# Another written order for the attention, gating and dispatch stage, and 34 in place of 48 idle products ahead of the first expert

## The chip, the cores and the metric

The kernel runs on one core of one Trainium2 chip. The metric is the device time of one execution in microseconds (us), the median of several runs. The engines of the core are TensorE (PE; its weight loads are listed apart as PEld), VectorE (DVE), ScalarE (ACT), GpSimd (POOL) and SyncE (SP), which here only issues transfers. Each engine takes its instructions in the order in which they stand in its queue, and a wait at the head of a queue holds everything behind it.

## What is computed

Three layers stand behind one another, all in fp32, on 2304 tokens of 512 features:

```python
# attention: 4 batches, 8 heads, 576 positions, head size 64, a window of 128 positions
scores = scale * q @ k.T + bias            # bias falls with the distance, outside the window -1e9
attn = exp(scores - max); attn /= attn.sum()
x = (attn @ v) as 2304 x 512

# experts: each token goes to one of 8
e_idx = argmax(x @ w_gate)
gate = softmax(x @ w_gate)[e_idx] * sigmoid(x @ w_output_gate)[e_idx]
x[e] = gate * (relu(x[e] @ w1[e]) @ w2[e])

# gated layer
out = (silu(x @ w_gate2) * (x @ w_val)) @ w_out
```

## The kernel before

**Stages.** The kernel works in three stages. The first (about 0 to 147 us) does attention, finds each token's expert, and writes each token's row to that expert's list in device memory (`xs`). The second computes the experts one after another, the third the gated layer. The change touches the first stage and the step from it to the first expert.

**The written order.** The first stage runs over 18 blocks `j` of 128 tokens, each in two halves of four heads (`j.hf`), and over 9 pairs of blocks `u`. Its order isn't left to a scheduler: the string `ORDER` (L28) lists 617 steps, and the loop under `manual_schedule` (L807) issues them one by one. So each engine's queue holds its part of the steps in the order of the string. A step is a letter and its place:

- `q`, `i`, `v`, `R`, `z` are transfers on SP: rows of q and k, of v, of the first expert's weights, and zeros into `xs`.
- `T` turns q and k (PE, tile `tq`), `Q` copies them out of PSUM (tile `qk`), `S` makes the scores (PE, tile `s`), `C` selects those inside the window and `M` adds the bias (DVE), `E` takes the exponentials (four on ACT), `P` turns them (PE, tile `tp`), `p` copies them out (tile `pt`), `K` masks them on POOL (`affine_select`, tile `ptm`), `V` multiplies by the values (PE, tile `o`), and `x` copies the result out (tile `xt`).
- `N` makes the reciprocal sums. `G`, `l`, `F`, `f` make the gating logits (PE, copy, PE, DVE). For six groups of blocks, `g` picks the expert, `e` takes two exponentials, `b` counts the tokens of the group (its first instruction writes `gs`), `w` makes the weights, `r` (PE) and `k` (DVE) the token's place (`gsli`).
- `t` turns the attention result back to rows (PE, tile `tx`), `X` scales the rows (DVE, tile `xtok`), `a` appends the token's number, and `D` (POOL, L769) writes a block's rows to their places with an indirect transfer.
- `H` (ACT) and `L` (POOL, L795) split a weight tile of the first expert into a high and a low part.

**A star** behind `Q`, `p`, `x` or `l` puts that copy on DVE in place of ACT (L807 to L811); behind another letter it means nothing.

**The hand-over.** After the last step, L1416 to L1431 issue in this order: the load of the first expert's rows (`load_x(0)`, tile `xr`, on SP), which waits until all 18 `D` have landed; `expert_tables`, a count of the tokens of each expert (PE, tile `cnt_ps`, L854) and a chain of small DVE instructions on it; products of a tile of ones that nobody reads, held behind the last count (`keep_warm`); five parts of `token_order`, which lengthen the DVE chain; and `emit_xT(0)`, which turns the first expert's rows (PE, L1063), copies the high part (ACT, `xh`, L1064) and subtracts the low part (DVE, `xl`, L1065). The first expert's products (L1440) take `xh` four times, then `xl` four times, then `xh` four times for each slice of the result.

Of the kernel before, what the change touches and what calls it, by code (L numbers as in the profile page):

```python
# [25 lines left out]


ORDER = """  # L28
q0 i0 q1 T0.0 a2 B1 Q0.0 q2 S0.0 B0 T0.1 C0.0 Q0.1 q3 T1.1 M0.0 S0.1 Q1.1 E0.0 T1.0 C0.1 q4 T2.0 Q1.0 S1.1 M0.1
Q2.0 E0.1 T2.1 C1.1 S1.0 v0 M1.1 T3.1 Q2.1 C1.0 E1.1 P0.1 q5 P0.0 M1.0 S2.1 p0.1 S2.0 Q3.1 K0.1 T4.1 p0.0 C2.0  # L30
v1 P1.1 E1.0 K0.0 C2.1 T3.0 V0.0 R0 M2.0 V0.1 Q3.0 R1 M2.1 E2.0 S3.0 q6 S3.1 C3.0 p1.1 T5.1 x0* Q4.1 K1.1 P1.0
M3.0 Q5.1 T4.0 q7 p1.0 P2.0 N0 Q4.0 T5.0 K1.0 C3.1 E2.1 S4.0 M3.1 V1.0 C4.0 q8 Q5.0 p2.0 V1.1 M4.0 E3.1 K2.0
S5.0 T6.0 v2 C5.0 E3.0 S4.1 T6.1 R2 C4.1 Q6.0 P2.1 v3 x1* Q6.1 P3.0 p2.1 T7.0 M5.0 p3.0 P3.1 K2.1 R3 M4.1 E4.0
T7.1 S5.1 v4 K3.0 S6.0 C5.1 Q7.0 z0 p3.1 G0 N1 H0 C6.0 P4.0 K3.1 l0 M5.1 V2.0 E4.1 v5 V2.1 p4.0 M6.0 S6.1 v6
E5.0 K4.0 x2* S7.0 C6.1 q9 F0 Q7.1 P4.1 f0 E5.1 T8.0 V3.0 C7.0 g0 V3.1 Q8.0 R4 p4.1 P5.1 q10 E6.0 M7.0 K4.1 P5.0
T8.1 M6.1 S7.1 L0* H1 x3* p5.1 S8.0 C7.1 v7 Q8.1 r0 p5.0 b0 T9.0 E6.1 N2 P6.0 R5 K5.0 M7.1 V4.0 q11 C8.0 V4.1
Q9.0 K5.1 k0 E7.0 G1 x4* S8.1 M8.0 q12 e0 P6.1 l1 C8.1 p6.0 T9.1 p6.1 P7.0 M8.1 Q9.1 t1 K6.1 E8.0 T10.0 w0 q13
S9.1 S9.0 C9.1 Q10.0 K6.0 V5.0 E7.1 R6 X1 V5.1 L1* M9.1 H2 R7 P7.1 p7.0 L2* v8 x5* F1 H3 T10.1 C9.0 p7.1 S10.0
K7.0 E9.1 R8 G2 v9 f1 V6.0 K7.1 Q10.1 V6.1 l2 z1 M9.0 E8.1 L3* T11.1 x6* F2 P9.1 f2 Q11.1 S10.1 p9.1 v10 H4 t0
K9.1 C10.1 E9.0 P8.0 z2 X0 P8.1 a3 V7.0 C10.0 L4* H5 M10.0 V7.1 p8.1 E10.0 v11 g1 S11.1 T12.1 z3 K8.1 C11.1 p8.0  # L40
T11.0 Q12.1 P9.0 M10.1 Q11.0 P10.0 K8.0 H6 T12.0 x7* S11.0 p10.0 R9 M11.1 L5* H7 V8.0 q14 C11.0 H8 Q12.0 a0 V8.1
N3 p9.0 M11.0 L6* e1 t5 E11.0 x8* G3 K9.0 z4 S12.1 w1 E10.1 S12.0 X5 T13.0 b1 R10 l3 T13.1 C12.0 L7* H9 F3 q15
V9.0 E11.1 f3 V9.1 N4 K10.0 C12.1 Q13.0 P11.0 Q13.1 M12.1 z5 T14.1 L8* p11.0 P10.1 x9* Q14.1 T14.0 H10 t2 M12.0
a1 L9* S13.0 p10.1 X2 Q14.0 R11 S13.1 E12.1 K10.1 z6 t3 C13.1 T15.0 K11.0 C13.0 P11.1 E12.0 V10.0 M13.0 L10* R12
V10.1 p11.1 X3 R13 H11 N5 P12.0 x10* Q15.0 z7 L11* T15.1 p12.0 M13.1 P12.1 Q15.1 S14.0 K12.0 E13.1 S15.0 C14.0
q16 G4 K11.1 C15.0 p12.1 V11.0 l4 M15.0 H12 K12.1 V11.1 E13.0 M14.0 v12 L12* r1 F4 P13.1 H13 f4 q17 S15.1 p13.1
D1 k1 E14.0 S14.1 g2 P13.0 D0 T16.1 p13.0 v13 T16.0 x11* Q16.1 P14.0 K13.0 C15.1 E15.0 G5 R14 C14.1 V12.0 K13.1
v14 M15.1 e2 V12.1 l5 D5 Q16.0 w2 v15 P15.0 p14.0 T17.0 M14.1 K14.0 p15.0 t4 R15 Q17.0 F5 S16.1 v16 H14 D2 N6 f5
x12 S17.0 E14.1 v17 V13.0 C16.1 K15.0 M16.1 V13.1 E15.1 L13* C17.0 S16.0 X4 L14* P14.1 x13 C16.0 P15.1 p14.1 r2
D4 b2 p15.1 t8 k2 G6 X8 a4 t7 K15.1 l6 M16.0 t6 E16.0 F6 V15.0 D3 f6 X6 V15.1 E16.1 a6 K14.1 X7 T17.1 M17.0  # L50
P16.0 Q17.1 D7 t9 g3 p16.0 P16.1 x15 S17.1 D8 p16.1 b3 V14.0 E17.0 N7 C17.1 K16.0 V14.1 X9 P17.0 K16.1 M17.1 x14
r3 e3 p17.0 t10 D9 w3 E17.1 t13 V16.0 X13 D6 k3 G7 N8 P17.1 l7 X10 K17.0 t11 p17.1 t12 X11 H15 F7 K17.1 V16.1
X12 f7 a5 D13 x16 g4 V17.0 e4 D10 V17.1 b4 w4 r4 x17 D11 t15 k4 G8 X15 t14 a7 L15* l8 F8 X14 t17 a8 f8 t16 D15
g5 e5 D14 b5 r5 w5 D12 X16 k5 X17 D16 D17
""".split()


# [89 lines left out]
def attn_moe_glu_kernel(ctx, tc, q, k, v, w_gate, w_ogate, w1, w2, w2_gate, w2_val, w2_out, out, caps=CAPS):  # L147
# [66 lines left out]
    with ExitStack():  # L214
# [610 lines left out]
        ps_m = wctx.enter_context(tc.tile_pool(name="ps_m", reuse_waits="tile", bufs=8, space=PSUM))  # L825
# [241 lines left out]
        yr, x2 = {}, {}  # L1067
# [314 lines left out]
        S_P5, S_P1, S_U2, V1, V2, G1, SG1, SG2 = range(8)  # L1382
# [237 lines left out]
```

## Time and profile before

| what | before |
|---|---|
| median of 3 runs | 804.83 us (803.99 to 805.16) |
| the profiled execution | 804.16 us |
| its span, first to last instruction | 802.0 us |
| mean granted TensorE clock | 0.993 |
| instructions | 17462 |
| PE busy | 777.6 us (97%) |
| DVE busy | 667.0 us (83%) |
| ACT busy | 504.7 us (63%) |
| POOL busy | 115.2 us (14%) |

The span leaves out 2.16 us of the profiled execution's own time, and this execution lies 0.67 us under the median. Shares of the whole span say little on the first stage, which is less than a fifth of it; so the rows below are of stretches. In a row of the timeline the number in brackets is the time that the engine had been idle before the instruction, with what ended that. Ends of PE's products are modelled, and a PE that is busy may be one that waits inside a group.

### The profile page before, as it was taken

Reading aid. Unit: us, or ns where it says so; the run is one execution under the profiler, and the core shown is the slowest. Engines: PE = TensorE matmul, PEld = TensorE weight load, DVE = VectorE, ACT = ScalarE, POOL = GpSimd, SP = SyncE. Lnnn points to the kernel's source line nnn. Section 1 sums busy time; section 2 is a strip of 40 time slices with the busy share of each in tenths; the row PEclk is TensorE's granted clock in tenths of the full one; section 3 lists DMA queues with packets and bytes.
Section 4 is the critical chain, followed back from the end, with each engine's and each line's share of the span. In section 5 each row is a group of like instructions: output and inputs, shape, how many; then the busy total and the mean of one; then the engine's idle time right before and its main releaser. Section 6 shows DMA issues by size and latency. Waiting matters only on the chain.

```text
span 802.0 us, 17462 instructions
## 1 busy us (share of the span) xinstructions
PE 777.6 (97%) x6031; PEld 720.7 (90%) x6031; DVE 667.0 (83%) x1808; ACT 504.7 (63%) x1355; POOL 115.2 (14%) x212
## 2 busy tenths in 40 slices
PE   8999998999999999999999999999999999999994
PEld 6888785799999999899899999999999999999993
DVE  8799787696798898889999999999877898777643
ACT  6999883266566677768776766665544665455431
POOL 5466787000000000000000000040000002000003
PEclk9999999999999999999999999999999999999998
DMA  9989943798868789990343221223110113011102
GB/s 181 242 200 309 292 132 125 228 309 244 253 216 259 232 287 291 278 335 27 127 135 109 99 93 52 71 114 131 54 51 28 54 54 131 28 52 53 52 29 81
DMA packets 120815, 121.16 MB, mean 151 GB/s; under 512 B 63634, under 2 KB 79634, under 8 KB 120722
## 3 DMA queue, kind: packets, MB, share of 16 engines
q1 hardware_dynamic: 113184, 106.31, 44.6%
q0 software_dynamic: 2880, 9.48, 3.1%
q10 hardware_dynamic: 4658, 4.20, 1.5%
q8 instruction: 49, 0.80, 0.4%
q14 instruction: 44, 0.36, 0.1%
HBM read 89.23 MB, written 30.73 MB: 150 GB/s over the span
## 4 chain that ended last, share of the span: by engine, by line
PE 40%; issue 34%; DVE 11%; ACT 6%; DMA 4%; POOL 2%; ACTq 1%; DVEq 0%; POOLq 0%; SPq 0%
PE pa L1312 7%; PE oo L1335 6%; PE oh L1440 5%; PE pb L1312 5%; PE oy L1464 4%; PE o L612 3%; DVE w L462 2%; PE s L521 2%; POOL out_dram L1350 2%; DMA rawd<-in_moe_w_gate_dram 2%; ACT w L461 2%; PE tp L589 1%; PE oy L1253 1%; PE oh L1232 1%; DVE t L1087 1%
## 5 line engine op out<-in xcount | busy, mean ns | idle before, releaser
L1335 PE MATMUL oo<-xh,hw 128*128 128x512 f32 x432 | 133.3, 390 | 0.0
L1312 PE MATMUL pa<-w 128*128 128x384 f32 x630 | 127.8, 338 | 0.8 <-ACT wtmp L1173 0.6
L1312 PEld LDWEIGHTS pa<-w 128*128 128x128 f32 x630 | 112.2, 188 | 9.4 <-ACT wtmp L1173 1.3
L1350 POOL DMA_INDIRECT out_dram<-ob,oid x18 | 20.5, 1137 | 631.9 <-ACT ob L1173 506.8
L1464 PE MATMUL oy<-hh,w 128*128 128x384 f32 (+5 forms) x448 | 101.1, 312 | 0.0
L1312 PE MATMUL pb<-w 128*128 128x384 f32 x468 | 94.5, 336 | 0.0
L1335 PEld LDWEIGHTS oo<-xh,hw 128*128 128x128 f32 x432 | 79.6, 187 | 6.4
L1173 ACT ACTIVATE w<-w 128x256 fp32r<-128x256 f32 (+2 forms) x168 | 76.2, 461 | 14.2 <-DVE w L1200 10.5
L1335 PE MATMUL oo<-xl,hw 128*128 128x512 f32 x216 | 84.4, 391 | 0.0
L1312 PEld LDWEIGHTS pb<-w 128*128 128x128 f32 x468 | 82.7, 188 | 0.4 <-DVE wtmp L1388 0.3
L462 DVE TENSOR_TENSOR w<-raw,w 128x512 fp32r<-128x512 f32 x112 | 75.1, 678 | 8.2 <-ACT w L461 6.6
L1440 PE MATMUL oh<-xh,w 128*128 128x384 f32 (+5 forms) x448 | 79.1, 316 | 0.0
L1173 ACT ACTIVATE wtmp<-pa 128x384 f32<-128x384 f32 x72 | 35.4, 492 | 65.0 <-PE pa L1312 64.8
L1464 PEld LDWEIGHTS oy<-hh,w 128*128 128x128 f32 x448 | 75.8, 188 | 0.0
L461 ACT ACTIVATE w<-raw 128x512 fp32r<-128x512 f32 x112 | 67.6, 622 | 8.5 <-ACT y L1107 5.3
L1440 PEld LDWEIGHTS oh<-xh,w 128*128 128x128 f32 x448 | 70.5, 192 | 0.6 <-ACT xh L1064 0.4
L1173 ACT ACTIVATE w<-wraw 128x256 fp32r<-128x256 f32 x108 | 44.5, 414 | 41.7 <-PE pa L1312 26.1
L1464 PE MATMUL oy<-hl,w 128*128 128x384 f32 (+5 forms) x224 | 69.8, 312 | 0.0
L1388 DVE TENSOR_TENSOR wtmp<-pb,wtmp 128x384 f32<-128x384 f32 x72 | 40.1, 557 | 32.5 <-ACT wtmp L1173 26.4
L1385 DVE TENSOR_TENSOR wtmp<-wtmp 128x384 f32<-128x384 f32 x108 | 58.5, 554 | 6.1 <-ACT wtmp L1391 5.4
L575 ACT ACTIVATE p<-p,mn 128x128 f32<-128x128 f32 x144 | 55.9, 401 | 0.5 <-DVE mn L554 0.3
L1221 DVE TENSOR_TENSOR w<-wraw,w 128x256 fp32r<-128x256 f32 x108 | 44.3, 419 | 6.3 <-ACT w L1173 6.3
(258 smaller groups left out, 1609.8 us busy)
## 6 DMA issues: line engine op xcount, KB each, us to landing
raw<-in_moe_w_dram SPq DMA_DIRECT2D x128, 256.0 KB, 3.8
xs<-zrow SPq DMA_DIRECT2D x8, 774.0 KB, 7.2
rawd<-in_moe_w_gate_dram SPq DMA_DIRECT2D x24, 256.0 KB, 4.4
rawd<-in_moe_w_val_dram SPq DMA_DIRECT2D x24, 256.0 KB, 3.4
rawd<-in_moe_w_out_dram SPq DMA_DIRECT2D x24, 256.0 KB, 3.7
xh<-wo_s SPq DMA_DIRECT2D x24, 256.0 KB, 2.6
xl<-wo_s SPq DMA_DIRECT2D x24, 256.0 KB, 2.8
w<-ys SPq DMA_DIRECT2D x6, 768.0 KB, 7.5
```

What stands on the lines that cost most here:

```text
L461: nc.scalar.activation(out=s[:, 0, :], in_=t, func=AF.Copy)
L462: TT(out=s[:, 1, :], in0=t, in1=s[:, 0, :], op=ALU.subtract)
L575: last_exp[0] = nc.scalar.activation(out=pr[:, c, :], in_=pr[:, c, :], func=AF.Exp, bias=mn[:, c:c + 1], scale=-1.0, accum_out=sums[j][:, ...
L1173: nc.scalar.activation(out=out, in_=in_, func=AF.Copy)
L1221: TT(out=flat(w_at(s, j)[:, 1]), in0=w_src(s, j), in1=flat(w_at(s, j)[:, 0]), op=ALU.subtract)
L1312: nc.tensor.matmul(out=bank_of(j), lhsT=w[:, a, k, :], rhs=x_at(j, b, k), start=(n == 0 and j in (0, 1, 5)), stop=(n == 5), skip_group_che ...
L1335: nc.tensor.matmul(out=o_w[c], lhsT=h_at(s, t)[b][:, b0 * 128:b0 * 128 + 128], rhs=wo_at(s, a), start=(kk == 0 and i == 0), stop=(kk == KF ...
L1350: r = nc.gpsimd.indirect_dma_start(out=out[:, :], out_offset=bass.IndirectOffsetOnAxis(ap=oid[:, 2 * WB * pr + c, :], axis=0), in_=ob, in_ ...
L1385: TT(out=out, in0=a, in1=b, op=ALU.mult)
L1388: TT(out=temp(i), in0=bank_of(j), in1=temp(k), op=ALU.add)
L1440: nc.tensor.matmul(out=o[:, 0:n], lhsT=wt["w1", p, m // 4, kk][:, a, (m % 4) * 128:(m % 4) * 128 + 128], rhs=(xh, xl)[b][:, kk, :], start= ...
L1464: nc.tensor.matmul(out=o[d][:, 0:n], lhsT=wt["w2", p, 0, kk][:, a, d * 128:d * 128 + 128], rhs=(hh, hl)[b][:, kk, :], start=(kk == 0 and i ...
```

## The change

The string `ORDER` is written anew, with the same 617 steps in another order, and with stars on other copies: before, 12 copies are on DVE (`x0` to `x11`); after, 24 are (nine `Q`, nine `p`, `x2`, `x5`, `x8`, `x12`, `l2`, `l5`). Nothing is added or left out. The number of idle products goes from 48 to 34.

```diff
 ORDER = """
-q0 i0 q1 T0.0 a2 B1 Q0.0 q2 S0.0 B0 T0.1 C0.0 Q0.1 q3 T1.1 M0.0 S0.1 Q1.1 E0.0 T1.0 C0.1 q4 T2.0 Q1.0 S1.1 M0.1
+q0 i0 q1 T0.0 Q0.0 q2 T0.1 S0.0 Q0.1 S0.1 a3 C0.0 B0 v0 T1.1 M0.0 T1.0 Q1.1 q3 E0.0 C0.1 S1.1 a0 a2 T2.0 C1.1
...
-g5 e5 D14 b5 r5 w5 D12 X16 k5 X17 D16 D17
+D14 r5 t17 b5 D12 X16 k5 X17 D16 D17 L13* L14* L15*
 """.split()
...
         with tc.issue_after(last_cnt[0]):
-            keep_warm(ps_m, "m", 48)
+            keep_warm(ps_m, "m", 34)
```

Of POOL's queue, these are the last rows of the stage. `xs<-xtok,gsli` is a `D`, `w<-raw,w` an `L`, `apart` a small write that stands between two `D`, `zcols` the first instruction of the hand-over. Before:

```order
L642 COPY xtok<-pads 128x2x4
L795 TENSOR_TENSOR w<-raw,w 128x512
L642 COPY xtok<-pads 128x2x4
L769 DMA xs<-xtok,gsli 18433x516
L768 MEMSET apart 1x1
L769 DMA xs<-xtok,gsli 18433x516
...
L769 DMA xs<-xtok,gsli 18433x516
L837 MEMSET zcols 128x1664
```

and after:

```order
L642 COPY xtok<-pads 128x2x4
L769 DMA xs<-xtok,gsli 18433x516
L768 MEMSET apart 1x1
L769 DMA xs<-xtok,gsli 18433x516
...
L769 DMA xs<-xtok,gsli 18433x516
L795 TENSOR_TENSOR w<-raw,w 128x512 x3
L837 MEMSET zcols 128x1664
```

The last three splits (`L13` to `L15`) stood ahead of `D`s before, one of them five `D`s before the end; now all three run behind the last `D`.

On ACT, the end of the stage: `xt<-o` is an `x`, `lt<-g` an `l`, `w<-raw` an `H`, `geo` and `pe` an `e`. Before:

```order
L504 ACTIVATE xt<-o 128x4x128
L504 ACTIVATE lt<-g 128x256
L715 ACTIVATE geo<-lg 128x16
L716 ACTIVATE pe_209<-gsh 128x2x8
L1419 ACT_TABLE_LOAD
```

and after:

```order
L504 ACTIVATE xt<-o 128x4x128 x2
L786 ACTIVATE w<-raw 128x512 x2
L504 ACTIVATE lt<-g 128x256
L715 ACTIVATE geo<-lg 128x16
L716 ACTIVATE pe_209<-gsh 128x2x8
L1419 ACT_TABLE_LOAD
```

Two splits (`H14`, `H15`) now stand between the last `x` and the last `l`.

On DVE, the last group's gating, from the choice of the expert to the counts of the hand-over (`gs` and `gbase` are of `b`, `pe` to `gwi` of `w`, `xtok` is an `X`, `grk` to `gsli` are `k`). Before:

```order
L709 TENSOR_TENSOR gohb<-iota8m,gmn 128x16
L725 TENSOR_REDUCE gs<-gohb 128x8
L727 TENSOR_TENSOR expf<-gmn,iota8m 128x2
L729 TENSOR_TENSOR gbase<-expf,rows_e 128x2
L757 TENSOR_TENSOR pe_209<-gohb,geo 128x2x8
...
L762 TENSOR_TENSOR gwi<-inv,gwgt 128x16
L683 TENSOR_TENSOR xtok<-tx,gwi 128x512
```

and after:

```order
L709 TENSOR_TENSOR gohb<-iota8m,gmn 128x16
L757 TENSOR_TENSOR pe_209<-gohb,geo 128x2x8
...
L762 TENSOR_TENSOR gwi<-inv,gwgt 128x16
L725 TENSOR_REDUCE gs<-gohb 128x8
L727 TENSOR_TENSOR expf<-gmn,iota8m 128x2
L729 TENSOR_TENSOR gbase<-expf,rows_e 128x2
L683 TENSOR_TENSOR xtok<-tx,gwi 128x512
```

The group's count `gs`, on which the count of all tokens and with it the idle products wait, moves behind the five instructions of the weights. What follows (`L683` to the counts of the hand-over) is the same in both.

## Rows read from the trace of the kernel before

**Rows 1.** Busy time by stretch: PE, PEld, DVE, ACT, POOL, granted clock, DMA share, GB/s.

```profile
0.00:20.00 20.00, 17.07 (x276) 12.46 (x280) 16.67 (x80) 13.41 (x47) 10.28 (x55) 1.00 0.99 181
20.00:60.00 40.00, 39.52 (x819) 34.37 (x809) 33.93 (x165) 39.48 (x156) 22.34 (x32) 1.00 0.94 221
60.00:80.00 20.00, 19.31 (x339) 16.32 (x336) 18.86 (x73) 18.23 (x63) 13.97 (x20) 1.00 1.08 309
80.00:138.00 58.00, 52.46 (x858) 41.82 (x859) 46.54 (x208) 40.12 (x144) 43.69 (x66) 1.00 0.61 185
150.00:310.00 160.00, 160.00 (x1027) 159.52 (x1026) 132.01 (x301) 101.21 (x231) 0.00 (x0) 1.00 0.84 261
```

**Rows 2.** The chain of waits in the first stage: start, length, what.

```profile
11.52 0.96 ACT qk L504 x2
...
61.34 0.70 DVE s L542
...
115.90 1.79 DVE gbase L729
```

**Rows 3.** Groups by line and shape, 0 to 138 us: busy us, mean ns | idle before.

```profile
L504 ACT ACTIVATE qk<-tq 128x512 f32<-128x512 f32 x36 | 20.9, 592 | 5.4 <-PE tq L495 5.4
L786 ACT ACTIVATE w<-raw 128x512 fp32r<-128x512 f32 x16 | 10.0, 630 | 1.3 <-DMA raw<-in_moe_w_dram 1.3
L506 DVE COPY xt<-o 128x512 f32<-128x512 f32 x12 | 8.2, 686 | 0.6 <-PE o L612 0.5
```

**Rows 4.** Timeline of DVE and POOL at 72 to 77 us, gating of one group.

```profile
72.71 1.23 POOL L278 TENSOR_SCALAR_AFFINE_SELECT ptm<-pt 128x512 f32<-128x512 f32 x2
72.81 0.18 DVE L760 RECIPROCAL gwgt<-gwgt 128x4 f32<-128x4 f32 x1
...
73.90 1.27 POOL L795 TENSOR_TENSOR w<-raw,w 128x512 fp32r<-128x512 f32 x1
...
74.22 0.98 DVE L727 TENSOR_TENSOR expf<-gmn,iota8m 128x4 f32<-128x4 f32 x1
...
75.23 1.33 DVE L729 TENSOR_TENSOR gbase<-expf,rows_e 128x4 f32<-128x4 f32 x1
75.27 1.27 POOL L795 TENSOR_TENSOR w<-raw,w 128x512 fp32r<-128x512 f32 x1
```

**Rows 5.** Timeline of PE and ACT at the last values product.

```profile
126.26 1.97 PE L612 MATMUL o<-ptm,vr 128*64 128x128 f32 x32 [0.79 <-ACT geo L715]
...
129.81 0.60 ACT L504 ACTIVATE xt<-o 128x512 f32<-128x512 f32 x1 [3.23 <-PE tx L680]
...
131.17 0.38 ACT L504 ACTIVATE lt<-g 128x256 f32<-128x256 f32 x1 [0.76 <-PE g L648]
```

**Rows 6.** Timeline of the hand-over to the first expert, 134 to 150 us.

```profile
134.74 10.52 PE L250 MATMUL warm<-ones 128*128 128x512 bf16 x48
...
137.33 0.96 POOL L769 DMA_INDIRECT xs<-xtok,gsli  x1 [1.69 <-DVE gsli L750]
...
138.59 0.96 POOL L769 DMA_INDIRECT xs<-xtok,gsli  x1 [0.21 <-DVE reg L862]
139.57 0.94 DVE L876 TENSOR_TENSOR end<-end,held 128x1 f32<-128x1 f32 x5
...
146.16 1.69 PE L1063 MATMUL tx<-ident,xr 128*128 128x128 f32 x12 [0.90 <-DMA xr<-xs]
146.70 0.30 DVE L910 TENSOR_REDUCE lim<-tbl 128x18 f32<-128x144 f32 x1
...
147.32 1.95 DVE L1065 TENSOR_TENSOR xl<-tx,xh 128x384 fp32r<-128x384 f32 x4 [0.32 <-ACT xh L1064]
...
148.78 0.99 PE L1440 MATMUL oh<-xl,w 128*128 128x384 f32 x4
```

**Rows 7.** Busy time and granted clock around two pauses of PE, columns as Rows 1.

```profile
328.00:330.00 2.00, 0.41 (x3) 0.24 (x3) 1.97 (x5) 2.00 (x6) 0.00 (x0) 1.00 0.68 216
330.00:332.00 2.00, 2.00 (x12) 2.00 (x12) 1.97 (x5) 1.17 (x4) 0.00 (x0) 0.55 1.12 221
332.00:334.00 2.00, 2.00 (x13) 2.00 (x13) 0.31 (x1) 0.41 (x2) 0.00 (x0) 0.59 1.04 240
354.00:356.00 2.00, 0.79 (x7) 0.63 (x6) 1.97 (x6) 2.00 (x8) 0.00 (x0) 1.00 1.06 395
```

More of the change, by code (lines that the diff above doesn't have):

```diff
@@ L28 @@
 ORDER = """
-q0 i0 q1 T0.0 a2 B1 Q0.0 q2 S0.0 B0 T0.1 C0.0 Q0.1 q3 T1.1 M0.0 S0.1 Q1.1 E0.0 T1.0 C0.1 q4 T2.0 Q1.0 S1.1 M0.1
[L30 to L53, printed above, removed]
@@ L54 @@
-g5 e5 D14 b5 r5 w5 D12 X16 k5 X17 D16 D17
+q0 i0 q1 T0.0 Q0.0 q2 T0.1 S0.0 Q0.1 S0.1 a3 C0.0 B0 v0 T1.1 M0.0 T1.0 Q1.1 q3 E0.0 C0.1 S1.1 a0 a2 T2.0 C1.1
+Q1.0 P0.0 Q2.0 q4 T2.1 M0.1 E0.1 M1.1 S1.0 p0.0* S2.0 Q2.1 C1.0 R0 E1.1 K0.0 P0.1 C2.0 T3.1 q5 T3.0 M1.0 V0.0
+Q3.1 p0.1 P1.1 M2.0 E2.0 K0.1 S3.1 p1.1* q6 S2.1 Q3.0* K1.1 E1.0 V0.1 C2.1 T4.0 B1 C3.1 T4.1 Q4.0 v1 M2.1 P1.0
+Q4.1 P2.0 E2.1 M3.1 T5.0 R1 S3.0 p2.0* q7 S4.0 C3.0 Q5.0 T6.0 p1.0 C4.0 T5.1 K1.0 Q6.0 M3.0 P2.1 x0 T6.1 v2 M4.0
+E3.0 S4.1 K2.0 p2.1* S5.0 q8 Q6.1* K2.1 E4.0 V1.0 C4.1 V1.1 M4.1 E3.1 P4.0 R2 Q5.1* T7.0 C5.0 R3 P3.0 H0 S5.1 N0
@@ new lines @@
+x1 v3 p3.0* L0* H1 V2.0 C5.1 p4.0 v4 E4.1 M5.0 V2.1 K4.0 M5.1 S6.1 q9 K3.0 H2 Q7.0* S6.0 E5.0 C6.1 G0 L1* x2*
+T7.1 R4 l0 C6.0 P4.1 Q7.1 P3.1 R5 M6.1 p4.1 P5.0 p3.1 T8.0 z0 N1 E5.1 T8.1 M6.0 K3.1 S7.0 Q8.0* S7.1 K4.1 p5.0
+Q8.1* T9.0 E6.0 q10 C7.0 P5.1 L2* C7.1 F0 V3.0 Q9.0 M7.0 E6.1 V3.1 f0 v5 S8.0 g0 p5.1 R6 T9.1 x3 P6.1 K5.1 C8.0
+E7.0 v6 P6.0 M7.1 V4.0 K5.0 v7 p6.0* Q9.1 V4.1 e0 M8.0 K6.0 p6.1 v8 S9.0 x4 w0 E7.1 S8.1 q11 C9.0 T10.0 K6.1
+T10.1 Q10.0 P7.1 C8.1 Q10.1 P7.0 H3 V5.0 p7.1* q12 H4 L3* M9.0 V5.1 E9.0 M8.1 a1 S9.1 L4* x5* p7.0 R7 S10.1 C9.1
@@ new lines @@
+E8.0 K7.1 G1 q13 G2 V6.0 K7.0 H5 l2* C10.1 l1 E8.1 V6.1 N3 v9 M9.1 F2 P8.0 N2 E9.1 T11.0 f2 R8 S10.0 z1 p8.0*
+P9.0 Q11.0 C10.0 K8.0 T12.0 p9.0 M10.1 T12.1 Q12.0 T11.1 L5* x6 M10.0 F1 R9 S11.0 E10.0 Q11.1* v10 K9.0 S12.0
+Q12.1* V7.0 E10.1 f1 q14 V7.1 g1 e1 P10.0 x7 P8.1 C11.0 p10.0 T13.0 q15 b0 p8.1 P9.1 M11.0 H6 t0 K8.1 V8.0 E11.0
+X0 K10.0 C12.0 V8.1 z2 Q13.0 M12.0 S12.1 p9.1 E12.0 w1 S11.1 T14.0 R10 K9.1 C12.1 P10.1 Q14.0 z3 C11.1 t1 p10.1
+P12.0 X1 T14.1 K10.1 p12.0 M12.1 t5 Q14.1 P11.0 H7 M11.1 L6* r0 z4 S13.0 E12.1 x8* S14.0 b1 V9.0 k0 E11.1 R11 N4
@@ new lines @@
+V9.1 K12.0 C13.0 v11 p11.0 T13.1 X5 L7* P12.1 C14.0 Q13.1 q16 t3 p12.1 M13.0 T15.1 H8 r1 K12.1 M14.0 S14.1 H9 x9
+S13.1 N5 E13.0 z5 C14.1 L8* V10.0 X3 V10.1 k1 K11.0 E14.0 G3 z6 Q15.1* G4 l3 C13.1 L9* P13.0 H10 M14.1 P11.1 l4
+p13.0 t4 L10* p11.1 T15.0 z7 X4 t2 Q15.0 K11.1 M13.1 P14.0 x10 F3 S15.0 H11 f3 E13.1 v12 S15.1 L11* C15.0 V11.0
+C15.1 q17 p14.0 V11.1 M15.1 K13.0 T16.1 X2 x11 K14.0 T16.0 M15.0 Q16.1 P13.1 R12 Q16.0 F4 D4 N6 S16.1 E15.0 R13
+f4 S16.0 v13 g2 D0 G5 e2 E15.1 V12.0 v14 l5* D5 b2 V12.1 w2 v15 H12 D1 T17.1 p13.1 x12* P15.1 Q17.1 R14 T17.0
@@ new lines @@
+C16.1 K13.1 p15.1 r2 v16 Q17.0 P15.0 k2 E14.1 D2 F5 V13.0 f5 R15 V13.1 M16.1 a4 v17 p15.0 a6 K15.1 E16.1 P14.1
+C16.0 t6 D3 N7 t9 M16.0 x13 S17.0 p14.1 X9 K15.0 S17.1 E16.0 C17.0 G6 X6 L12* P16.1 C17.1 l6 P16.0 p16.1 K14.1
+t8 M17.1 H13 V15.0 E17.1 M17.0 a5 V15.1 K16.1 p16.0* t7 X8 x15 K16.0 F6 E17.0 V14.0 X7 f6 D9 V14.1 g3 e3 P17.1
+D6 x14 P17.0 p17.1 b3 G7 p17.0 w3 D8 t11 l7 t10 X11 r3 K17.0 X10 F7 V16.0 f7 D7 V16.1 k3 g4 t13 e4 t15 x16 t12
+X13 K17.1 V17.0 X12 D11 w4 V17.1 X15 t14 x17 a7 D10 r4 N8 H14 G8 X14 H15 b4 t16 l8 a8 k4 F8 D13 f8 g5 D15 e5 w5
```

## The prediction

> **What bounds the kernel now.** I read the busy time by stretch first [rows 1]. From 150 us on PE is busy all the time (160.00 of 160), so a delay or gain at the first expert passes to the end in full; what remains is the first stage and the hand-over. Up to 80 us the transfers take 0.94 to 1.08 of what the DMA engines have, and the compute engines are nearly full too: from 20 to 60 us PE 39.52 and ACT 39.48 of 40, DVE 33.93; from 60 to 80 us PE 19.31, DVE 18.86, ACT 18.23 of 20. Only the first 20 us (PE idle 2.9) and the end, 80 to 138 us (PE idle 5.5, counting idle products as work), have room. Then the chain of waits [rows 2]: early it runs over ACT (a piece is `qk`, 0.96 for two copies), later over DVE (`s`, and `gbase`, an instruction on 128x4 numbers that took 1.79 us). Last the hand-over [rows 6]: the last `D` is issued at 138.59, the expert's rows are there at 146.16, and the small DVE chain that began beside it ends at 147.00 (146.70 + 0.30), 0.32 us ahead of the first `xl`. So the DVE chain and the load end almost together.
>
> **The change part by part.** (1) Copies. Nine `Q` and nine `p` leave ACT, eight `x` come back, two `l` leave: 18 x 0.59 - 8 x 0.59 + 2 x 0.38 = 6.7 us less on ACT [rows 3, 5]. DVE gets ten more at 0.686 and two smaller at some 0.4: 7.7 us more. So the load isn't made smaller, it moves from an engine that was full early to one that had 85% in the stretch from 20 to 60 us. By their place in the string (an estimate, steps counted against the stretches) three of the 24 starred copies fall in the first 20 us, 13 in the 40 us after it (6 before), four in the next 20 (four before), four behind that (two before). In the first 20 us ACT makes the chain, and three copies less are worth up to 3 x 0.59 = 1.8 us, while DVE has 3.3 us of room: taken as -1.2. From 20 to 60 us seven more copies cost DVE 7 x 0.6 = 4.2 us of its 6.07 idle, and PE can't go faster than 39.52 of 40: 0. From 60 to 80 us nothing. Behind that the order sets the exponentials and value products against the row work anew; PE has 5.5 us of idle time there, of which a good part is the latency of the last blocks; nothing in the trace shows the new waits. Nearest bounds: all of PE's idle time in the stage goes (-6, some of it can't), or half of DVE's ten extra copies land where DVE makes the chain (+3). Taken: -0.8, nearer to nothing, since the work is the same. Parts of SP's queue move too (`v0`, `q3`, the zero fills); their sum is the same and DMA is full to 80 us either way; in the value above. Sum of (1): **-2.0**, from -6 to +3.
>
> (2) The end of attention. Two weight splits of 0.63 us on ACT now stand between the last `x` and the last `l` [rows 3]. Before, `l` began 0.76 us after `x` ended (129.81 + 0.60 to 131.17), the time of the product between them [rows 5]; now it can't begin before 2 x 0.63 = 1.26: **+0.5**. The last value products end at 128.23, and their copy begins only at 129.81 [rows 5]; the 1.58 us between have no cause that I see and may not come again: between 0 and -1.6, half taken, **-0.7**.
>
> (3) The three splits behind the last `D`. For the `D`s it is a gain of 3 x 1.27 us of POOL, but POOL waited 1.69 us for DVE ahead of the last two `D`s [rows 6], so that is worth 0. Behind them it costs. DVE instructions with two operands in SBUF stand still while POOL works on SBUF data [rows 4]: `expf` took 0.98 us and ended with POOL's split (73.90 + 1.27 = 75.17), `gbase` 1.33 us and ended with the next (75.27 + 1.27 = 76.54). The three splits run from the end of the last `D` (138.59 + 0.96 = 139.55 in before's time) for 3.8 us, just where DVE's chain does `end` (five in 0.94 us, undisturbed [rows 6]) and more of the kind. If one passes at the end of each split, the chain gets on by 3 x 0.19 = 0.6 us in 3.8, and loses 3.2. It had 0.32 us of slack, so the four `xl` come **2.9 us** later, and PE's second pass, which takes `xl` from 148.78 on [rows 6], with them. Queued behind on DVE: the `xl`, then the first `hl`; who waits is PE. Bounds: 0, if such narrow operands slip through, and 3.8 - 0.3 = 3.5, if none passes.
>
> An instruction with one operand ran at its usual length beside POOL, `gwgt` 0.18 us under a POOL instruction that began at 72.71 [rows 4]. The Trainium skill, GPSIMD Engine Reference, section Key points, says that GpSimd shares its SBUF interfaces with VectorE and gets in the way of instructions with two SBUF inputs and also of those in a two-port mode. By it single-operand copies of the chain might be held as well, which would give the upper bound, 806.0 in place of 805.4; the row with 0.18 us speaks against that here.
>
> (4) 34 idle products. One is 10.52 / 48 = 0.219 us [rows 6]. The group's count now stands behind five small instructions (0.94 us for five such), so the products begin 1.0 us later against the `D`s, and 34 of them end at 134.74 + 1.0 + 7.45 = 143.2 in place of 145.26. They don't hold the path either way. But PE then pauses about 3.0 us ahead of the first transposes in place of 0.90, and again for the `xl`. After a pause with 0.41 us of work in 2 the granted clock fell to its lower level (1.2 GHz) for (0.45 + 0.41) x 2 / 0.5 = 3.4 us, half of which is lost work, 1.7 us; a pause of 1.2 us at 354 us left it up [rows 7]. Here the slow products would lie partly under the wait for `xl`: from 0 to 1.7, taken **+0.5**.
>
> The Trainium skill, TensorE: Matmul & The Clock Gate, Part 1, says that the low clock is the default and that activity holds it up, which makes a fall after the shorter run of products likely; by that alone the term would be 1.7 and the time 806.6. The rows show both outcomes.
>
> Sum on the profiled execution: 804.16 - 2.0 + 0.5 - 0.7 + 2.9 + 0.5 = **805.4**. The median before is 804.83, 0.67 above that execution, so this is no more than 0.6 us above it.
>
> **The rivals.** A: the new order closes the pauses of the first stage, as far as PE's idle time goes, -6 in place of -2.0: 801.4. For it speaks that ACT was full for 40 us and is relieved by 6.7 us, and that DVE lost time on held gating instructions (`gbase`, 1.79 us [rows 2]) which other neighbours on POOL would spare; against it, that PE was full there too. It decides if the last value product comes 5 us earlier. B, on the other side: DVE becomes the bound. Its 7.7 us come on top of 46.54 of 58 us busy and 18.86 of 20 [rows 1]; if five copies fall on its chain, (1) is +3 in place of -2.0: 810.4. The place is the stretch from 60 to 138 us, and it decides if DVE is over 90% busy there. C: the splits behind the last `D` don't hold the DVE chain, since operands of 128x1 slip through; then nothing pauses PE for `xl`: 805.4 - 2.9 - 0.2 = 802.3. The change does do what it says, since the rows of the new order show each moved step.
>
> **How the numbers follow.** Chances: forecast 0.40, A 0.28, B 0.19, C 0.13. A measurement of this kernel can tell about 0.2%, 1.6 us. The forecast's own range is 802.3 to 808.0, by the bounds of (2) to (4), and holds 0.05 faster, 0.17 within, 0.18 slower. A gives 0.25 faster, 0.03 within; B 0.19 slower; C 0.08 faster, 0.04 within, 0.01 slower. Sum: faster 0.38, same 0.24, slower 0.38. No side holds a majority: the gain in (1) and the price in (3) are of one size. The range from 800.0 to 810.5 leaves out the far half of B and the best of A.
>
> **What would show it.** (1) The last value product ends 1 to 3 us earlier than 128.2, and ACT is no longer full from 20 to 60 us, DVE is at some 95%. (2) The last `l` begins over 1.2 us after the last `x`. (3) Rows of `end` on DVE take 0.5 to 1.3 us each while the three splits run, the chain ends some 3 us after the rows have landed, and PE waits for `xl` that long. (4) The idle products end about 3 us ahead of the transposes, and the granted clock in the next 4 us shows whether that costs. Wrong it is if DVE's chain of the hand-over has its old length, or if the first stage moves by more than 4 us either way.

## The result: slower by 1%

After the change the kernel took 813.12 us (median of 4 runs, 812.35 to 814.0) against 804.41 us before (4 runs, 803.93 to 805.16): a ratio of 1.0104, 95% interval 1.0089 to 1.0118. The forecast was 805.4 with a range to 810.5; the time lies 7.7 us above the one and 2.6 us above the other. (The ratio on record is not the quotient of the two medians, which is 1.0108.) The profiled execution took 812.35 us with a span of 810.3, which is 8.2 us more than the 802.0 before.

Busy time by stretch after the change (PE, PEld, DVE, ACT, POOL, then granted clock, DMA share, GB/s), in the stretches of [rows 1]:

```profile
0.00:20.00 20.00, 16.49 (x294) 12.16 (x295) 17.54 (x76) 13.31 (x49) 10.50 (x58) 1.00 1.12 188
20.00:60.00 40.00, 40.00 (x825) 35.29 (x824) 37.73 (x176) 38.78 (x155) 24.05 (x36) 1.00 1.03 229
60.00:80.00 20.00, 20.00 (x397) 18.25 (x399) 18.67 (x102) 19.06 (x69) 12.42 (x19) 1.00 1.09 300
80.00:138.00 58.00, 49.85 (x764) 39.91 (x757) 41.52 (x181) 34.02 (x123) 39.19 (x61) 0.90 0.60 180
150.00:310.00 160.00, 156.65 (x977) 155.42 (x978) 130.51 (x305) 96.47 (x219) 0.00 (x0) 0.98 0.80 250
```

Up to 80 us nothing speaks against the new order: ACT has a little room (38.78 of 40, 39.48 before), DVE is at 94%, PE runs through. Then two things show that were not there before. From 80 to 138 us the granted clock is 0.90 in place of 1.00, and PE has 2.6 us less busy time. And behind 150 us, where PE was full in [rows 1], 3.35 us are idle and the clock is 0.98.

The first is here, by the same columns:

```profile
92.00:94.00 2.00, 1.75 (x51) 1.41 (x50) 1.70 (x9) 2.00 (x11) 1.76 (x3) 1.00 0.86 172
94.00:96.00 2.00, 1.09 (x11) 0.53 (x12) 0.71 (x4) 2.00 (x12) 1.64 (x3) 1.00 0.99 333
96.00:98.00 2.00, 0.83 (x4) 0.29 (x2) 0.00 (x0) 0.85 (x2) 1.42 (x3) 0.54 0.99 278
98.00:100.00 2.00, 1.54 (x15) 0.53 (x14) 0.00 (x0) 0.00 (x0) 0.00 (x0) 0.50 1.17 318
100.00:102.00 2.00, 2.00 (x22) 1.92 (x20) 1.54 (x9) 0.00 (x0) 0.00 (x0) 0.50 1.12 352
```

PE's timeline in that stretch (start, length, operation, count, and in brackets the idle time before it with what ended that):

```profile
94.94 0.38 PE L521 MATMUL s<-qk 64*64 64x128 f32 x2 [0.50 <-issue]
95.73 0.29 PE L521 MATMUL s<-qk 64*64 64x128 f32 x1 [0.41 <-issue]
96.46 0.37 PE L521 MATMUL s<-qk 64*64 64x128 f32 x1 [0.44 <-issue]
97.19 0.35 PE L521 MATMUL s<-qk 64*64 64x64 f32 x1 [0.36 <-issue]
```

From 94 to 98.6 us PE takes one score product every 0.73 us, and the profile names nothing that it waits for ("issue"); DVE and ACT then run dry. The lower clock level (1.2 GHz) follows, and value products run at half speed: 3.37 us for 32 at 100.08 in place of the 1.97 of [rows 5].

The second is the hand-over, to be read against [rows 6]. POOL, DVE and PE:

```profile
137.42 0.97 POOL L769 DMA_INDIRECT xs<-xtok,gsli  x1 [1.47 <-DVE gsli L750]
138.69 0.97 POOL L769 DMA_INDIRECT xs<-xtok,gsli  x1 [0.22 <-DVE srt L859]
139.69 3.71 POOL L795 TENSOR_TENSOR w<-raw,w 128x512 fp32r<-128x512 f32 x3
143.34 1.48 POOL L837 MEMSET zcols<- 128x1664 f32 x1
...
139.14 5.72 DVE L867 CAST ep<-reg 128x8 f32<-128x8 int32 x1
143.35 1.51 DVE L868 CAST held<-ci 128x8 f32<-128x8 int32 x1
144.89 0.23 DVE L882 TENSOR_TENSOR tbl<-iota,ep 128x64 f32<-128x64 f32 x1
...
135.89 9.78 PE L250 MATMUL warm<-ones 128*128 128x512 bf16 x34
146.38 1.70 PE L1063 MATMUL tx<-ident,xr 128*128 128x128 f32 x12 [0.71 <-DVE end L876]
147.84 1.38 PE L1440 MATMUL oh<-xh,w 128*128 128x384 f32 x4
153.35 2.08 PE L1440 MATMUL oh<-xl,w 128*128 128x384 f32 x4 [4.12 <-DVE xl L1065]
```

The last `D` is issued at 138.69, 0.10 us later than before. Then a DVE instruction on 128x8 numbers takes 5.72 us: it ends at 144.86, when POOL's three splits and the memset behind them are over (143.40 and 144.82). The first `xl` starts at 152.75 in place of 147.32, and PE waits 4.12 us for it. The clock falls in that wait:

```profile
150.00:152.00 2.00, 0.00 (x0) 0.00 (x0) 1.73 (x10) 0.00 (x0) 0.00 (x0) 0.70 1.12 237
152.00:154.00 2.00, 0.65 (x2) 0.48 (x2) 1.93 (x6) 0.00 (x0) 0.00 (x0) 0.50 1.04 259
154.00:156.00 2.00, 2.00 (x7) 1.65 (x7) 0.68 (x2) 0.00 (x0) 0.00 (x0) 0.50 1.02 354
```

The 8.2 us split up by four events that both traces have (the last `D`, the first `xl`, the first product `oy`, the end):

| from, to | before | after | more |
|---|---|---|---|
| start to the last `D` | 138.59 | 138.69 | +0.10 |
| last `D` to first `xl` | 8.73 | 14.06 | +5.33 |
| first `xl` to the first expert's `oy` | 17.55 | 18.82 | +1.27 |
| from there to the end of the span | 637.2 | 638.7 | +1.5 |

So the new order brought nothing by the last `D`, and the stretch from there to the first `oy` lost 6.6 us. Two questions were left for experiments: what each late edit is worth, and whether the pauses at 94 us belong to the order.

### The profile page after: what moved, and what is told of

It reads as the page before. It is cut to its first block, busy times and chain, and to the rows that moved or that the text cites. A ratio compares the mean times of both kernels' runs of the same rounds, so it can differ in the third digit from the quotient of the medians.

```text
span 810.3 us, 17438 instructions
## 1 busy us (share of the span) xinstructions
PE 777.7 (96%) x6017; PEld 721.6 (89%) x6017; DVE 672.0 (83%) x1820; ACT 500.5 (62%) x1343; POOL 114.8 (14%) x213
## 4 chain that ended last, share of the span: by engine, by line
PE 45%; issue 35%; DVE 9%; DMA 4%; ACT 3%; POOL 2%; ACTq 1%; SPq 0%; DVEq 0%; POOLq 0%
PE pa L1312 7%; PE oo L1335 6%; PE oh L1440 6%; PE pb L1312 5%; PE o L612 4%; PE oy L1464 4%; PE s L521 4%; DVE w L462 3%; PE tp L589 2%; DMA rawd<-in_moe_w_gate_dram 2%; PE tq L495 2%; POOL out_dram L1350 2%; PE oh L1232 1%; DMA raw<-in_moe_w_dram 1%; PE oy L1253 1%
## 5 line engine op out<-in xcount | busy, mean ns | idle before, releaser
L1440 PE MATMUL oh<-xl,w 128*128 128x384 f32 (+5 forms) x224 | 44.4, 319 | 5.7 <-DVE xl L1065 4.1
```

The lines of the kernel that those rows point to most:

```text
L1440: nc.tensor.matmul(out=o[:, 0:n], lhsT=wt["w1", p, m // 4, kk][:, a, (m % 4) * 128:(m % 4) * 128 + 128], rhs=(xh, xl)[b][:, kk, :], start= ...
```

## Experiments

Ratios are against runs of the kernel before on the same chip in the same batch; 0.1% is 0.8 us. They are the ratios on record, which differ by up to 0.13% from the quotients of the medians (e3 1.0040 in place of 1.0028, g3 1.0031 in place of 1.0044). "Last `D` to first `xl`" is read from each run's own trace.

### One part at a time

**e1**: the new order and 34 products, with the splits `L13` to `L15` ahead of the last `D`, and `H14` and `H15`, which make their other half on ACT, earlier too. Of each line only the part with moved steps is shown.

```diff
-t8 M17.1 H13 V15.0 E17.1 M17.0 a5 V15.1
+t8 M17.1 H13 H14 V15.0 E17.1 M17.0 a5 L13 V15.1
...
-w3 D8 t11 l7 t10
+w3 D8 L14 t11 l7 H15 t10
...
-r4 N8 H14 G8 X14 H15 b4 t16 l8 a8 k4 F8 D13 f8
+r4 N8 G8 X14 b4 t16 l8 a8 k4 F8 D13 L15 f8
...
-D12 X16 k5 X17 D16 D17 L13* L14* L15*
+D12 X16 k5 X17 D16 D17
```

> The order of after, with the three splits L13 to L15 ahead of the last D as in before (in pauses of POOL at about 112, 120 and 129 us), and their H14 and H15 earlier too. Theory S (the splits behind the last D hold DVE's small chain, and the wait for xl then costs clock): the CAST of the hand-over (held, 5.72 us in after) is short again, the chain ends near 147.0, and 5.4 us and some 1.8 us of clock come back: 813.1 - 7.2 = 805.9, from 804.5 to 807. Theory O (the new order of attention is itself the loss): less than 2 us come back, over 811. Theory W (the shorter run of idle products costs the clock): 813 less 5.4, about 807.7, and the granted clock still falls behind 150 us.

Measured: 804.84 us, ratio 1.0028 (1.0006 to 1.0050). The CAST `ep` took 0.17 us again. Less than after, but not the level of before, and the chain wasn't as short as before either: last `D` to first `xl` was 11.1 us, not 8.7. DVE and POOL show why:

```profile
125.12 1.92 DVE L750 TENSOR_TENSOR gsli<-gbase,rankf 128x2 int32<-128x2 f32 x1
133.51 0.17 DVE L856 COPY cnt<-cnt_ps 128x8 f32<-128x8 f32 x1 [1.34 <-DMA xs<-xtok,gsli]
134.11 1.49 DVE L861 CAST ki<-srt 128x8 int32<-128x8 f32 x1
...
125.74 1.27 POOL L795 TENSOR_TENSOR w<-raw,w 128x512 fp32r<-128x512 f32 x1
134.07 1.50 POOL L837 MEMSET zcols<- 128x1664 f32 x1
```

A split that stands ahead of the last `D` holds DVE too (`gsli` 1.92 us, 0.16 where nothing is beside it). And in the new order `cnt`, the first instruction of the chain, waits 1.34 us for a row transfer to land, so that the CAST `ki` meets the memset and is held until that ends.

What `cnt` waits for isn't its own input, since it reads nothing of the rows (it copies a tile of counts, L856). In f1 the landing is that of block 12, the third-last `D` (issued at 128.78, landed at 132.15). In the old order the same instruction depends on the transfers of blocks 15 and 14, the fifth- and fourth-last, which have landed before DVE gets there. The row buffers come from a pool of four (L226), and the tile that `cnt` writes belongs to a pool that is opened (L824) once attention's pools are closed (L814). So `cnt` probably waits for the memory of a row buffer, and which blocks used that buffer last follows from the written order. This is read from the code; no run moved the buffer.

**e2**: the order of before with 48 products, and L13 to L15 behind `D17`.

```diff
-D12 X16 k5 X17 D16 D17
+D12 X16 k5 X17 D16 D17 L13* L14* L15*
```

> The order of before with 48 idle products, and L13 to L15 alone moved behind the last D. Theory S: the same instructions of the hand-over are held as in after, the first xl comes 5 us later, the clock falls behind 150 us; 804.4 + 5.4 + 1.8 = 811.6, from 809.5 to 812.5. Theory O: under 806, since the order of attention stays. Theory W: up to 807.5 (the prediction's own 2.9 for the splits and no loss of clock).

Measured: 806.10 us, ratio 1.0037 (1.0019 to 1.0055): about half of what was expected. The hold is there, whole, on a TENSOR_TENSOR this time:

```profile
134.68 4.32 DVE L882 TENSOR_TENSOR tbl<-iota,ep 128x64 f32<-128x64 f32 x1 [0.18 <-DVE held L868]
139.30 0.94 DVE L876 TENSOR_TENSOR end<-end,held 128x1 f32<-128x1 f32 x5
...
135.21 3.70 POOL L795 TENSOR_TENSOR w<-raw,w 128x512 fp32r<-128x512 f32 x3
138.86 1.48 POOL L837 MEMSET zcols<- 128x1664 f32 x1
```

Not one DVE instruction passed in the 3.70 us of the splits. The memset behind them didn't hold the five `end` (0.94 us, as in [rows 6]).

**e3**: after with 48 products.

```diff
-            keep_warm(ps_m, "m", 34)
+            keep_warm(ps_m, "m", 48)
```

> After, with 48 idle products again. Theory S: the pause that costs clock is the one for xl behind the transposes, which the products don't reach; 813.1, not more than 1 us less. Theory W: the products keep the clock up through the hand-over, 1.7 us or more come back, under 811.4.

Measured: 805.70 us, ratio 1.0028 (1.0006 to 1.0049). The first number expected was 813; but this was another chip than the first runs', and what after takes there was not known yet. A 4.19 us hold of `key` and a wait for `xl` of 3.8 us stood in the trace all the same. Against after on this chip (h1 below, 1.0055) the 48 products bring back 0.27%, 2.2 us, by the mark of theory W (1.7 or more) and not by that of S (no more than 1); the intervals of the two ratios are too wide to tell the two marks apart.

**e4**: before with 34 products, the reverse edit.

> Before, with 34 idle products. Theory S: PE pauses about 3.9 us ahead of the first transposes in place of 0.9, but never for xl; some clock may be lost in the transposes, 804.4 to 805.4. Theory W: 1.7 us or more lost behind it, over 806.

Measured: 805.43 us, ratio 1.0035 (1.0014 to 1.0057), more than theory S gave. PE:

```profile
131.04 7.50 PE L250 MATMUL warm<-ones 128*128 128x512 bf16 x34
142.55 2.53 PE L1063 MATMUL tx<-ident,xr 128*128 128x128 f32 x12 [4.01 <-DMA xr<-xs]
144.73 1.63 PE L1440 MATMUL oh<-xh,w 128*128 128x384 f32 x4
```

PE pauses 4.01 us ahead of the transposes; they take 2.53 us in place of 1.69 [rows 6] and the granted clock from 144 to 146 us is 0.50, its lower level. That is some 1 us in this trace (0.84 on the transposes, the rest on the first products); the median says 2.9, with 1.1 to 4.6 in the interval.

So four different combinations of the parts, one or two of the three at a time, each cost about 0.3%. None of the theories S, O and W had that.

### The rest of the square, and before and after themselves

**f1** is after, unchanged; **f4** is before, unchanged, for its trace.

> After once more, beside before on the chip on which its parts were taken apart. Four runs there gave 2.3 us for the order with 34 products and the splits ahead, 3.2 us for order and splits with 48 products, 2.9 us for 34 products in the old order, 3.6 us for the splits alone in the old order. Theory P (each late edit costs clock by its own pause, and a second one adds its full price): 1.010 of before or more, about 8 us. Theory Q (the late edits share one price, the new order gains some 2 us that the edits eat up): 1.004 to 1.007.

> Before once more, for its trace on this chip: the last D some 4 us earlier than in the first trace (138.59 there), DVE's chain of the hand-over at its usual length of 8.4 us from ep to the last lim, and no pauses of 0.3 to 0.5 us ahead of single score products near 94 us.

Measured: f1 807.17 us, ratio 1.0060 (1.0036 to 1.0083), not 1.0104; that is theory Q's range and under P's. f4 as expected: its last `D` 3.3 us earlier than in the first trace, the chain 8.4 us, no pauses. The rows of f4 and of f1 that answer [rows 5, 6] (the last values product, its copy, the last `D`, the first `xl`), f4 first:

```profile
123.59 1.97 PE L612 MATMUL o<-ptm,vr 128*64 128x128 f32 x32 [0.79 <-ACT geo L715]
125.60 0.60 ACT L504 ACTIVATE xt<-o 128x512 f32<-128x512 f32 x1 [1.69 <-PE o L612]
135.27 0.96 POOL L769 DMA_INDIRECT xs<-xtok,gsli  x1 [0.22 <-DVE reg L862]
143.83 1.95 DVE L1065 TENSOR_TENSOR xl<-tx,xh 128x384 fp32r<-128x384 f32 x4 [0.17 <-ACT xh L1064]
```

```profile
120.65 1.97 PE L612 MATMUL o<-ptm,vr 128*64 128x128 f32 x32
122.65 0.60 ACT L504 ACTIVATE xt<-o 128x512 f32<-128x512 f32 x1 [2.15 <-PE o L612]
131.88 0.97 POOL L769 DMA_INDIRECT xs<-xtok,gsli  x1 [0.21 <-issue]
146.61 1.94 DVE L1065 TENSOR_TENSOR xl<-tx,xh 128x384 fp32r<-128x384 f32 x4
```

Here the new order does gain: its last values product ends 2.9 us earlier and its last `D` is issued 3.4 us earlier (about 1 us of the latter is the moved splits, see step 3 below). There are no pauses at 94 us, and PE is busy 9.84 of 10 us from 90 to 100 (7.22 in the first trace of after). The 1.58 us between the last values product and its copy [rows 5] are gone as well, in both kernels. The hand-over takes the gain and more: 14.73 us from the last `D` to the first `xl` against 8.56.

**f2**: the new order alone (e1 with 48 products). **f3**: the old order with both late edits (e2 with 34 products).

> The new order alone: L13 to L15 ahead of the last D, and 48 products. If the new order of attention is a gain as the first profile after suggested up to 80 us: 1 to 3 us less than before. If it isn't: the same as before within 1 us. If the new order is itself a loss: over 2 us more.

> The old order with both late edits, splits behind the last D and 34 products. Theory P (the prices add up): 3.6 + 2.9 = 6.5 us more than before. Theory Q (one price for both, since PE pauses only once): 3.5 to 4.5 us more.

Measured: f2 803.96 us, ratio 1.0014 (0.9998 to 1.0030): no gain from the order. f3 806.98 us, ratio 1.0059 (1.0040 to 1.0078): the old order with both edits is as slow as after, and the prices add up in part (4.7 us by the ratio, between P's 6.5 and Q's 4.5). In f2 the last `D` is 2.3 us earlier than in f4 (132.93), and the first `xl` is not (144.00): the chain starts late and meets the memset, as in e1.

### Where the splits stand, and one split

**g1**: f2 with H13 to H15 together and all splits earlier (L13 behind `a5`, L14 behind `K16.0`, L15 behind `D8`). They were meant to run before about 118 us; the last of them ended at 121.5 us in g1 and at 119.6 in h2. **h2** is the same kernel on another chip.

> The new order with 48 products, H13 to H15 in one place and all three splits before about 118 us, so that none stands near the last blocks. In f2 the split L15 ran at 125.55 to 126.83, held gsli for 1.91 us in place of 0.17, and the last blocks' gating behind it. If that hold passes to the end: the last D 1.7 us earlier than in f2 (132.93), DVE's chain no more than 1 us longer than before's 8.4 us, and the time 1 to 2 us under f2's ratio of 1.0014, so 0.999 to 1.000 of before. If the lead is given back behind 310 us, as e4 and f2 show in part: 1.001.

> The new order with the splits early and 48 products once more. If it is really ahead of before: 0.998 to 0.9995 again. If the first ratio (0.9988, interval to 1.0003) was chance: 1.000 to 1.0015, as f2.

Measured: g1 802.25 us, ratio 0.9988 (0.9973 to 1.0003); h2 805.10 us, ratio 1.0017 (1.0003 to 1.0031). `gsli` was free again (0.16 us), but in both traces the chain still took 11.1 us. The two ratios lie on both sides of one: together they don't show the best arrangement found to be faster than before.

**g4**: after with only L15 behind the last `D`.

> After with L13 and L14 ahead again and only L15 behind the last D, 34 products. If DVE stands still for the whole of each split: 2 x 1.24 = 2.5 us less delay of the first xl than in after (one DVE instruction held for some 1.3 us by the split, and a CAST by the memset behind it for some 1.3), and PE's wait for xl near 2.5 in place of 5.0 us; 1.002 to 1.004 of before. If the three splits cost once, as one block: the wait stays over 4 us.

Measured: 805.24 us, ratio 1.0025 (1.0009 to 1.0040), as expected for splits that each cost their own length: the first `xl` comes 2.42 us sooner behind the last `D` than in f1, where 2.5 was expected.

```profile
133.27 1.27 POOL L795 TENSOR_TENSOR w<-raw,w 128x512 fp32r<-128x512 f32 x1
134.47 1.50 POOL L837 MEMSET zcols<- 128x1664 f32 x1
...
132.92 3.08 DVE L861 CAST ki<-srt 128x8 int32<-128x8 f32 x1
136.03 0.17 DVE L862 TENSOR_SCALAR reg<-ki 128x8 int32<-128x8 int32 x1
```

One CAST is held through the split and the memset. PE waited 2.2 us for `xl`. In the traces of these runs the time from the last `D` to the first `xl` then reads as a rule:

| order, splits behind the last `D` | last `D` to first `xl`, us |
|---|---|
| old, none (f4; h3, where the first `xl` also waits 0.87 for `xh`) | 8.56; 9.26 |
| old, three (e2, f3) | 12.41, 12.41 |
| new, none (e1, f2, g1, h2) | 11.1 in each |
| new, one (g4) | 12.31 |
| new, three (e3, f1, g3, h1) | 14.73 to 14.74 |

Four traces are not in the table: e4 (old, none) has 8.82, g2 (new, three) 14.74, and the first two, from another chip, 8.73 for before and 14.06 for after, where `cnt` waited only 0.36 us.

A split costs 1.2 to 1.3 us in either order, its own length on POOL. The new order costs 2.5 us by itself. In f4 `cnt` starts 1.0 us ahead of the last `D`:

```profile
134.25 0.15 DVE L856 COPY cnt<-cnt_ps 128x8 f32<-128x8 f32 x1
```

In the four traces of the new order without splits behind it starts 0.2 to 0.5 us behind it, after its wait for a row transfer (1.2 to 1.5 us later, against the last `D`); then `ki` is held by the memset for 1.2 to 1.6 us (0.17 us is its length where nothing is beside it). Each of the four traces loses 2.7 us by the two, of which 0.17 us was slack in f4, where the first `xl` waits that long for `xh`.

**g2**: after with the third and fourth row transfer later, against the pauses at 94 us.

```diff
-l5* D5 b2 V12.1 w2 v15 H12 D1 T17.1
+l5* b2 V12.1 w2 v15 H12 T17.1
...
-k2 E14.1 D2 F5
+k2 E14.1 D2 D5 D1 F5
```

> After with the third and fourth row transfer (D5, D1) moved behind the fifth (D2), so that two in place of four run back to back while the transfers are full. Where PE shows pauses of about 0.4 us ahead of single score products from 94 to 98.6 us, as in the first trace of after: if the four D cause them, they end near 95.5 us as in the first trace of before, and some 3 us come back with the clock. Where the run of after beside it shows no such pauses: the same time as after within 1 us.

Measured: 812.57 us, ratio 1.0120 (1.0100 to 1.0141). After beside it (g3) showed no pauses, so nothing was learnt on them, and the same time as after within 1 us was expected. It took 6.3 us more than g3's 806.24: the move itself made a new wait. DVE's waits from 88 to 112 us (waited for, us in total, times, longest):

```profile
DVE xtok L683 <- DMA xs<-xtok,gsli: 2.8, 1, 2.8
```

A scaled row block couldn't be written before an earlier one had left its buffer, PE stood still for 3.8 us behind that (in two pieces), and the clock fell.

### After, three times more

**g3** and **h1** are after again, **h3** before again.

> After on a further chip: 1.006 of before, if the 1.0104 of the first runs is owed to the pauses from 94 to 98.6 us and the clock behind them; 1.009 to 1.012 if it is the kernel's own.

> After on one more chip. If the pauses of PE from 94 to 98.6 us and the low clock behind them belong to the chip or the hour of the first runs: none of them here, the last value product ends near 120 to 124 us, and 1.004 to 1.006 of before. If they belong to the kernel and come back in some of its executions: 1.009 to 1.012, and the trace shows them again.

> Before once more, for its trace on this chip: the last D near 135 us as in f4, or near 138.6 us as in the first trace; the copy of the last value product right behind it (f4), or 1.58 us behind it (first trace).

Measured: g3 806.24 us, ratio 1.0044 (1.0027 to 1.0060); h1 807.95 us, ratio 1.0055 (1.0038 to 1.0072). h3's last `D` was issued at 135.94, near f4's. The pauses came back in none of the three later traces of after.

## Why the prediction was wrong

Of the change's three parts the runs form a full square (order, splits, products). By the later runs, with f1, g3 and h1 together as 1.0053 for after and f2 for the new order alone, moving the splits behind costs 0.14 to 0.37% (four pairs, mean 0.25%, 2.0 us), 34 products cost 0.14 to 0.35% (mean 0.24%, 2.0 us), and the order 0.14 to -0.09% (mean about 0). By quotients of medians the same three means are 0.26%, 0.17% (1.3 us) and about 0. Their sum, some 4 us, is what the later runs of after show, 3.5 to 4.8 us. Some of the pairs stand across two chips, each against its own runs of before; a single ratio has an interval of about 0.2% to either side, so the means are good to about 1 us.

Against the forecast of 805.4 for the profiled execution the first trace of after is 7.0 us too slow, and the table of the result says where: 2.3 by the last `D` (+0.1 in place of the -2.2 of steps 1 and 2), 2.4 from there to the first `xl` (+5.3 in place of the +2.9 of step 3), 0.8 to the first `oy` (+1.3 in place of the +0.5 of step 4), and 1.5 behind it, where nothing was forecast. So step (1) failed, step (3) had the size of its hold wrong, and step (4) was too small.

**Step (1), -2.0: failed.** The gain in attention exists in the later traces (2.3 us at the last `D` in f2 against f4, 1.8 to 2.7 in four pairs that differ by the order alone), near the size that was forecast; in the first trace the pauses at 94 us used it up. What the step left out is who uses it: the DVE chain of the hand-over, which the prediction took as starting with the last `D`s whatever the order. In the new order it starts 1.2 to 1.5 us later against them and runs into the memset; 2.5 us are gone and the first `xl` comes when it did. A gain ahead of the last `D` counts only as far as the chain behind it moves along.

**Step (2).** The two `H` between the last `x` and the last `l` cost less than was said. In the first trace of after the last `l` starts right behind the splits, 0.94 us after the last `x` ended, against 0.76 before: +0.2 in place of +0.5. In f1 it is 1.30 against 0.85 in f4, but there the splits had ended 0.26 us earlier, and what came last was the product that `l` copies (tile `g`), which had waited for DVE until 123.85:

```profile
124.55 0.38 ACT L504 ACTIVATE lt<-g 128x256 f32<-128x256 f32 x1 [0.26 <-PE g L648]
```

So where the right size shows, it comes from another wait, by luck. The -0.7 for the gap without a cause was nothing: the gap came again in the first trace of after (128.51 to 129.99), and is absent from the later traces of both orders.

**Step (3), +2.9.** The mechanism was right, the size of the hold was not: none of the DVE instructions passed, single-operand ones included, so the hold is 3.6 to 3.85 us in place of 3.2. What the prediction took from [rows 4], that an instruction with one operand slips through, holds for a RECIPROCAL beside an affine select; a CAST beside a split or a memset stood still (5.72, 3.08, 1.49 us). The memset behind the splits, which holds a CAST as well, was left out of the step altogether. The Trainium skill, GPSIMD Engine Reference, section Key points, names as its second condition an instruction in a two-port mode. The holds of the CASTs agree with it, and the prediction had set it aside for one row; but no row shows which mode a CAST ran in, so that this is the reason is not shown. The Trainium skill, Trainium Architecture — The Big Picture, section What this means for kernel authors, calls the sharing an exclusive lock, and the trace agrees: zero DVE instructions finished in 3.70 us. The prediction also gave nothing for the `D`s that come earlier; in the old order that is 1.0 us (e2 134.23 against f4 135.27). So the net delay of the first `xl` by this edit alone is 2.8 us (146.64 in e2, 143.83 in f4), which is the forecast's number by two errors of opposite sign.

**Step (4), +0.5.** Too small: the runs give 2.0 us by the ratios and 1.3 by the medians; whether that is above the step's own bound of 1.7 they don't tell. Part is seen: in e4 the transposes and the first pass at the lower clock, 1 us. In after the clock falls once more in the wait for `xl`, which the 34 products don't reach. The rest doesn't stand in single traces (the four pairs of profiled spans differ by +1.0, +1.2, +2.0 and -1.6 us), so where it lies is open.

**The premise.** The prediction took it that a delay or gain at the first expert passes to the end in full. In single traces it doesn't: in the old order the first `oy` of f3 comes 4.9 us after f4's and its span ends 2.0 us later, that of e2 4.4 and 0.8. Over the 17 traces the time from the first `oy` to the end is 636.4 to 641.2 us. Which waits behind the first expert make that difference was not followed.

**The range.** The bounds of (2) to (4) add up to 801.1 to 807.9; the 802.3 that is given as their lower end is C's time.

**What is left of the 1.0104.** The later runs of after, at 1.0044 to 1.0060, lie inside the range given (to 810.5, 1.0076 of the median before); the first ones don't. The last `D` of after was 6.8 us later in the first trace than in f1, that of before 3.3 us later than in f4. The difference of 3.5 us is about what lies between the two ratios, and the traces have it in one place: instruction by instruction after runs level with f1 (0.3 us) up to 94 us and is 6.8 us late at 103.5, before is 0.4 us behind f4 at 95.6 and 2.7 at 103.8. There lie the pauses from 94 to 98.6 us (2.8 us of waits in after, 0.9 in before) and the half clock behind them. Why PE got its products one by one there was not found. It fell together with the first row transfers of POOL while the transfers were full (share 0.99), in both kernels, for two `D`s in a row before and for four after; but f1 has the same four `D`s at the same times without a pause, and g2 couldn't test it. The cause stays open, and with it whether 8 or 4 us is the fairer price of this change.

**Rivals.** A, a gain of 6, had its mechanism half right (3.4 us at the last `D`). B's time is the nearest, but not its cause: DVE wasn't the bound in attention (23.5 of 30 us busy from 80 to 110 in f1). C is ruled out by `tbl`, 4.32 us.

## What to carry to other kernels

Time won in front of a hand-over counts only if the chain behind it starts earlier too; look up what that chain's first instruction waits for. Background work on POOL isn't free at such a place because POOL is idle: here each split stopped the DVE chain for its full length, on either side of the last transfer, and the memset did so where the chain stood at a CAST. Leave work of that kind where DVE has room. And measure the pair itself on more than one chip before you explain it, since the same two programs gave 1.0104 first and 1.0044 to 1.0060 later.

## What the runs showed of the hardware that was not expected

- A MEMSET of POOL (128x1664, 1.48 to 1.50 us) holds a CAST of DVE until it ends (1.19 us in f1, 1.49 in e1), but not a TENSOR_TENSOR of 128x1 (five in 0.94 us under it, e2 and [rows 6]).
- The size of the held instruction plays no part: 128x2 `gsli` (1.92 us), 128x8 CAST (5.72), 128x64 TENSOR_TENSOR (4.32) all waited for POOL's instruction to end.
- The hold begins in the traces before the record of the split does: `key` in f1 starts at 132.47 and the split at 132.88, `tbl` in e2 at 134.68 and 135.21, `ep` in after at 139.14 and 139.69, though the usual length of each is 0.17 to 0.23 us. Either POOL's start is recorded late or the hold begins earlier; no trace tells which.
- In f1 PE's wait of 5 us for `xl` was followed by granted clocks of 0.66, 0.50, 0.50 and 0.63 in the four stretches of 2 us from 146 to 154; in g1 and f4, with waits of 0.3 us or none, the clock stayed up there. After the 2.24 us in g4 it fell too (0.67 from 144 to 146 us), after the 1.25 us in e1 it did not.
